# Fused linear attention and feed-forward: PSUM as eight single banks, a filler bank, and a new order table

## The chip, the cores and the metric

The kernel runs on one NeuronCore of a Trainium2 chip. Its engines work side by side, each on its own list of instructions: TensorE (PE in the profile, with its weight loads as PEld), VectorE (DVE), ScalarE (ACT), GpSimd (POOL) and SyncE (SP, which here only starts transfers). TensorE writes its results to PSUM, 16 KB a partition in eight banks of 512 fp32 columns; DVE and ACT read them from there. POOL starts the loads from DRAM that change fp32 to bf16 on the way, SP the transposing transfers and the stores. The metric is the device time of one execution in microseconds.

## The reference

Attention over 8 batches, 8 heads, 576 positions and 64 columns a head, followed by a feed-forward layer over the 4608 rows that come out:

```python
def phi(x):
    proj = np.einsum('bhsd,df->bhsf', x, w_phi)                    # 64 -> 128
    proj = proj - np.max(np.abs(proj), axis=-1, keepdims=True)
    return np.concatenate([np.exp(proj), np.exp(-proj)], axis=-1)
q_p, k_p = phi(q), phi(k)
kv = np.einsum('bhsf,bhsd->bhfd', k_p, v)
z = np.sum(k_p, axis=2)
num = np.einsum('bhsf,bhfd->bhsd', q_p, kv)
den = np.einsum('bhsf,bhf->bhs', q_p, z)[..., None] + 1e-06
x = (num / den) as rows of 512                                     # 8 heads x 64
h = np.maximum(x @ w_in, 0.0)                                      # 512 -> 2048
out = h * h @ w_out                                                # 2048 -> 512
```

## The kernel before

Each batch's K goes through TensorE as 18 blocks of 128 positions in five groups (four of four blocks, one of two, the "rest" of 64 positions a head). The projection `e_kp` (L660) of a group uses half the array's rows for each of two heads. DVE takes the largest absolute value of each row (L595), ACT the two exponentials of either sign (L602) into `kph`. The maximum becomes a factor `em`, by which V is multiplied on DVE (L755, `va`; L738, `var` for the rest). `e_kv` (L776, L781) sums keys times values into `kvs`, eight heads and two signs a batch. Q is projected twice: `e_qm` (L878) for its maximum (DVE, L925) and `e_qp` (L888) for its exponentials (ACT, L915). `e_nd` (L970, and L978 for the rest, which uses half the array's columns) gives numerator and denominator, `e_t` (L1009, L1013 and others on DVE) brings the two signs together in `tmp`, then follow a reciprocal and a multiplication into `xo`.

`xo` is transposed to `xT`: on TensorE (L1083, with a copy out of PSUM) for batches 0 and 1, by a DMA transpose on SP's queue from batch 2 on (L1065, L1068). K and Q themselves go the same way (L630 and L840 on TensorE for batches 0 and 1, L566 and L570 by DMA after that). The feed-forward part runs in chunks of one tile of 128 rows (the first four) or two: `e_hp` (L1133) fills one bank with a group of the first layer, `e_hr` takes the positive part (ACT L1151 or DVE L1153), `e_sq` squares it (ACT L1161 or DVE L1163), `e_op` (L1189) is the second layer, `ot` its copy to SBUF.

PSUM is divided into three tiles `pj` of two banks and two tiles `mo` of one bank. Projections, sums and numerators of whole batches live in `pj`; transposes, the feed-forward and batch 0's sums live in `mo`. A matmul group that writes a tile waits until the last reader of its former content is done.

No planner runs in the kernel. Each piece of work is entered in a list by `add` (or `issue`, two entries for a transfer: start and landing), and `ORDER` gives the sequence in which the entries are emitted; every engine then works through its own part of that sequence. A minus sign takes the second engine that the entry allows. `WARM` gives filler matmuls that stand ahead of an entry (units of 128 columns), written into the tile that the entry is about to use; `e_fill` adds 40 units, and `e_first` 24 at the very start. Without `e_fill`'s own entry, which is not used, `WARM` has 44.

The loads of batch 0 go out on POOL's queue in this order: two pairs of K heads, V whole, the identity matrix (made by POOL itself), K's rest, V's rest, the first half of Q's columns, two parts of w_in, the second half of Q, two parts of w_in, Q's rest; then, once `ones` of batch 0 is done, batch 1's K, the two halves of w_out, and batch 1's Q and V. The other four K heads come in fp32 through SP's queue and are cast. A load waits for a free buffer, and on POOL's queue a transfer also waits for the eighth before it to land.

## Time and profile before

| | us |
|---|---|
| median of 3 runs (lowest, highest) | 360.85 (360.31, 361.56) |
| span of the profiled execution | 358.4 |
| the profiled execution's own time beside its span | not recorded apart from it |
| TensorE busy in the span | 346.4 |
| DVE, ACT, POOL busy in the span | 292.4, 262.9, 58.5 |

The runs time the whole execution; the span goes from the first to the last instruction of one profiled execution, so the median is 2.4 us above it. "Busy" counts the time in which at least one instruction of an engine runs; consecutive instructions overlap a little, so the mean length of one is more than what the next waits for, and the distance from start to start is read from the timeline. The granted clock is TensorE's, as a share of full speed.

### The profile page before, as it was taken

What the parts mean: (1) busy time and instruction counts of PE and PEld (TensorE: products, weight loads), DVE (VectorE), ACT (ScalarE), POOL (GpSimd) and SP (SyncE); (2) the same over time, 40 slices, a digit from 0 to 9 for tenths busy, and PEclk for the clock granted to TensorE, in tenths of its full rate; (3) what the DMA queues carried; (4) which work ended last, traced back from release to release, by engine and by line L of the source; (5) the groups of instructions that cost most, each with busy time, mean ns of one, the idle gap of its engine ahead of it and who ended that gap; (6) DMA issues with size and microseconds to landing.
All of it is one profiled execution on the core that took longest, in us unless ns stands there. A gap on an engine that the chain in (4) does not pass through costs nothing.

```text
span 358.4 us, 9254 instructions
## 1 busy us (share of the span) xinstructions
PE 346.4 (97%) x3860; PEld 239.1 (67%) x3894; DVE 292.4 (82%) x529; ACT 262.9 (73%) x436; POOL 58.5 (16%) x88
## 2 busy tenths in 40 slices
PE   8699999999999999999999999999999999999995
PEld 4378667775776676767576757757685768576754
DVE  5979998889998998788988699979988988591310
ACT  4979997996798774698849883798879867544641
POOL 8643323442160113100220002000000000000000
PEclk9969999999999999999999999999999999999999
DMA  9999999999997499607982194435203001113011
GB/s 161 185 197 207 194 208 141 170 181 187 186 152 138 83 171 150 107 15 145 124 126 53 59 149 96 61 89 82 60 16 88 18 35 48 65 34 88 2 59 59
DMA packets 92281, 39.33 MB, mean 110 GB/s; under 512 B 59728, under 2 KB 87760, under 8 KB 92240
## 3 DMA queue, kind: packets, MB, share of 16 engines
q0 software_dynamic: 42752, 18.09, 42.7%
q1 hardware_dynamic: 49328, 20.59, 28.6%
q8 instruction: 30, 0.49, 0.6%
q10 hardware_dynamic: 160, 0.07, 0.1%
q14 instruction: 11, 0.09, 0.1%
HBM read 36.77 MB, written 9.44 MB: 129 GB/s over the span
## 4 chain that ended last, share of the span: by engine, by line
PE 82%; DVE 8%; ACT 7%; issue 1%; POOL 1%; ACTq 0%; POOLq 0%
PE mo L1133 32%; PE mo L1189 31%; PE pj L781 4%; PE pj L970 4%; ACT kph L602 4%; PE pj L878 3%; PE pj L888 2%; DVE m L595 2%; PE pj L660 2%; DVE tmp L1009 1%; ACT hr L1151 1%; PE pj L776 1%; PE mo L781 1%; DVE va L755 1%; DVE hr L1153 1%
## 5 line engine op out<-in xcount | busy, mean ns | idle before, releaser
L1133 PE MATMUL mo<-xT,win 128*128 128x256 bf16 (+1 forms) x1280 | 139.3, 262 | 0.8 <-ACT hr L1151 0.2
L1189 PE MATMUL mo<-wout,h 128*128 128x512 bf16 (+1 forms) x558 | 131.2, 373 | 1.8 <-issue 0.2
L1133 PEld LDWEIGHTS <-win 128*128 128x128 bf16 x1280 | 111.3, 98 | 19.7 <-issue 4.3
L1189 PEld LDWEIGHTS <-h 128*128 128x128 bf16 x592 | 54.5, 98 | 57.3 <-issue 2.8
L915 ACT ACTIVATE qph<-pj 128x1024 bf16<-128x1024 f32 (+1 forms) x80 | 72.8, 940 | 11.6 <-PE pj L888 11.6
L1151 ACT ACTIVATE hr<-mo 128x512 bf16<-128x512 f32 x99 | 58.7, 598 | 28.2 <-PE mo L1133 27.0
L602 ACT ACTIVATE kph<-pj 128x1024 bf16<-128x1024 f32 (+1 forms) x80 | 71.2, 949 | 6.4 <-PE pj L660 4.9
L1163 DVE TENSOR_TENSOR h<-hr 128x512 bf16<-128x512 bf16 x82 | 33.7, 419 | 22.6 <-ACT hr L1151 22.0
L925 DVE TENSOR_REDUCE mq<-pj 128x8 f32<-128x1024 f32 (+1 forms) x40 | 44.2, 1108 | 4.5 <-PE pj L878 4.4
L595 DVE TENSOR_REDUCE m<-pj 128x8 f32<-128x1024 f32 (+1 forms) x40 | 44.3, 1111 | 3.4 <-ACT kph L602 1.7
L1161 ACT ACTIVATE h<-hr 128x512 bf16<-128x512 bf16 x62 | 38.9, 631 | 8.3 <-DVE hr L1153 7.5
L755 DVE TENSOR_TENSOR va<-vin,em 128x512 bf16<-128x512 bf16 x63 | 40.2, 683 | 0.1
L1153 DVE TENSOR_SCALAR hr<-mo 128x512 bf16<-128x512 f32 x45 | 30.6, 684 | 7.9 <-PE mo L1133 7.4
L417 ACT ACTIVATE ot<-mo 128x512 f32<-128x512 f32 (+1 forms) x24 | 14.0, 585 | 25.1 <-PE mo L1189 25.1
L1009 DVE TENSOR_TENSOR tmp<-pj,e 128x520 f32<-128x520 f32 x31 | 21.1, 692 | 6.1 <-PE pj L970 6.1
L970 PEld LDWEIGHTS <-qph 128*128 128x128 bf16 x512 | 21.9, 98 | 5.4 <-issue 1.5
L1042 DVE TENSOR_TENSOR xo<-tmp,rden 128x512 bf16<-128x512 f32 (+1 forms) x39 | 24.3, 631 | 0.5
L970 PE MATMUL pj<-kvs,qph 128*128 128x65 bf16 x512 | 24.4, 194 | 0.2
L781 PEld LDWEIGHTS <-kph 128*128 128x128 bf16 x512 | 21.5, 101 | 0.3
L1013 DVE TENSOR_TENSOR tmp<-pj,tmp 128x520 f32<-128x520 f32 x31 | 21.2, 692 | 0.5 <-PE pj L970 0.4
L781 PE MATMUL pj<-va,kph 128*128 128x65 bf16 x448 | 18.4, 194 | 0.0
L467 POOL DMA_DIRECT2D vin<-in_v_dram x8 | 7.2, 895 | 68.5 <-DVE va L755 63.1
(75 smaller groups left out, 268.5 us busy)
## 6 DMA issues: line engine op xcount, KB each, us to landing
out_dram<-ot SPq DMA_DIRECT2D x31, 256.0 KB, 2.4
vin<-in_v_dram POOLq DMA_DIRECT2D x8, 512.0 KB, 9.0
kin<-in_k_dram POOLq DMA_DIRECT2D x7, 512.0 KB, 11.9
qin<-in_q_dram POOLq DMA_DIRECT2D x7, 512.0 KB, 10.3
win<-in_moe_w_in_dram POOLq DMA_DIRECT2D x4, 512.0 KB, 10.1
...
xT<-xo SPq DMA_TRANSPOSE x36, 2.6
```

The source lines that it names most:

```text
L595: nc.vector.tensor_reduce(out=st["m"].rearrange("p (n c) -> p c n", c=2)[:, :, n0 : n0 + n], in_=st["pj", g][:, :, :n], axis=AX.X, op=ALU. ...
L602: nc.scalar.activation(out=st["kph"][:, s, n0 : n0 + n].rearrange("p n c f -> p c n f"), in_=st["pj", g][:, :, :n], func=ACT.Exp, scale=1. ...
L755: nc.vector.tensor_tensor(out=st["va"][:, s, gs, 0:D], in0=tiles["v", b].rearrange("p h i d -> p (h i) d")[:, gs, :], in1=st["em"][:, s, g ...
L781: nc.tensor.matmul(out=kv[:, sum_of(h) - 2 * prs[0], :], lhsT=st["kph"][:, s, 2 * h + i // 2, i % 2, :], rhs=st["va"][:, s, h * NI + i, :] ...
L915: nc.scalar.activation(out=st["qph", pt][:, s, half, n0 : n0 + n], in_=in_, func=ACT.Exp, scale=1.0 - 2.0 * s)
L925: nc.vector.tensor_reduce(out=st["mq", pt][:, half, n0 : n0 + n], in_=in_, axis=AX.X, op=ALU.max, apply_absolute_value=True)
L970: nc.tensor.matmul(out=nps[:, n + 4 * (ab or 0), :], lhsT=qph[:, s, half, sl, :], rhs=kvs[:, s, sum_of(sl), :], start=True, stop=True)
L1133: nc.tensor.matmul(out=hp[:, mi, :], lhsT=win[:, kc, mc * P : (mc + 1) * P], rhs=st_x[c][:, kc, 0:nt, :], start=kc == kcs[0] and (ab is No ...
L1151: nc.scalar.activation(out=out_, in_=in_, func=ACT.Relu)
L1153: nc.vector.tensor_scalar(out=out_, in0=in_, scalar1=0.0, scalar2=None, op0=ALU.max)
L1161: nc.scalar.activation(out=out_, in_=hr, func=ACT.Square)
L1189: nc.tensor.matmul(out=st["op"], lhsT=hst["h2"][:, mc, tt * P : (tt + 1) * P], rhs=wout[:, mc, cols], start=(mc == 0), stop=(mc == KC2 - 1))
```

## The change

- **PSUM.** `r_pj` and `r_mo` become one ring `r_ps` of eight single banks. All that took a two-bank tile takes two banks: K's and Q's projections, with one reduction and one exponential a sign for each bank; the sums in two halves of four heads; the numerators in groups of four heads. `e_qm` and `e_qp` are entries of their own in all batches, so that the table may place them apart.
- **Fillers.** `e_first` takes one bank, `spare`, which goes back to the ring with the first group of the first layer. All fillers are matmuls into that bank. `e_fill` goes; `WARM` has 187 units, all ahead of the first layer.
- **w_phi** comes in one transfer that doubles it over the partitions; `w2` has one plane, one cast, and no clearing.
- **Batch 0's loads.** POOL's queue: identity, K heads, V in two halves of four heads, V's rest, first half of Q, two parts of w_in, second half of Q, two parts of w_in, Q's rest, batch 1's K. Then come the seven multiplications that POOL now does in batch 0 (in the table's order: `va` negative sign groups 2, positive 2, one half of `var`, `va` positive 3, negative 0, 1 and 3), then K's rest of batch 1, w_out, batch 1's Q and V. K's rest of batch 0 comes in fp32 on SP's queue and is cast. The second set of loads no longer waits for `ones`. The first sum of batch 0 needs the first three of the seven, the last sum all seven.
- **Batch 1's `xo`** goes by DMA transpose like the later ones (`PE_X` names batch 0 alone).
- **Squares** are taken of two groups at once (1024 columns), except in the last chunk; `r_hr` has three double buffers.
- **`load_gate`**: from batch 3 on, the loads of a batch wait for the first `xo` of two batches before, by a small copy on POOL into `mark`.
- **`e_one`** may run on ACT instead of DVE.
- **`ORDER`** has 2084 entries instead of 1718. Of its relus ACT has 107 (99 before) and DVE 37 (45); of its squares ACT has 43 (62) and DVE 33 (82).

The diff, cut:

```diff
-WARM = {44: 7, 54: 10, 58: 6, 62: 2, 74: 13, 93: 4, 117: 5, 139: 2, 149: 8}
+WARM = {47: 3, 57: 6, 49: 1, 64: 9, 51: 1, 71: 22, 85: 30, 134: 21, 139: 13, 138: 12, 148: 14, 147: 8, 110: 1, 112: 3, 189:
+    4, 197: 13, 158: 1, 217: 3, 166: 2, 176: 3, 170: 11, 172: 6}
...
-    XB_IN, XB_X = 2, 2
+    XB_IN, PE_X = 2, [(0, pt, half) for pt in range(3) for half in range(2)]
...
-    r_pj = Ring("pj", 3, [P, 2, 4, P], F32, pool=ps)
-    r_mo = Ring("mo", 2, [P, 4, P], F32, pool=ps)
+    r_ps = Ring("ps", 8, [P, 4, P], F32, pool=ps)
...
-    r_hr = Ring("hr", 4, [P, 512], BF16)
+    r_hr = Ring("hr", 3, [P, 2, 512], BF16)
...
-        for half in range(2):
-            nc.scalar.dma_start(out=wst[half * Dh : (half + 1) * Dh], in_=w_phi)
+        nc.scalar.dma_start(out=wst, in_=w_phi.unsqueeze(0).to_broadcast([2, Dh, Fd]))
...
     def e_first(op):
-        warm(r_pj.tile(op)[:, 0], WARM_UP, zero)
...
+        spare["t"] = r_ps.tile(op)
+        fill(WARM_UP, zero)
+
+    def fill(n, with_):
+        for m in [4] * (n // 4) + ([n % 4] if n % 4 else []):
+            nc.tensor.matmul(out=spare["t"][:, :m], lhsT=with_, rhs=with_.unsqueeze(1).to_broadcast([P, m, P]),
                              start=True, stop=True)
...
+                o, d = plan.issue("sw", 1, key, {"pool": (0.92, 0.95)}, emit_v, "half", (), [] if o_v else [r_in["v"].slots],
+                                  after=[o])
...
+            for par in range(2):
+                lock = Lock()
+
+                def e_red(op, g=g, n0=n0, n=n, par=par):
+                    nc.vector.tensor_reduce(
+                        out=st["m"].rearrange("p (n c) -> p c n", c=2)[:, par, n0 : n0 + n], in_=st["pj", g, par][:, :n],
+                        axis=AX.X, op=ALU.max, apply_absolute_value=True)
...
+                for s in range(2):
+                    def e_exp(op, g=g, n0=n0, n=n, par=par, s=s):
+                        nc.scalar.activation(out=st["kph"][:, s, n0 : n0 + n, par, :], in_=st["pj", g, par][:, :n],
+                                             func=ACT.Exp, scale=1.0 - 2.0 * s)
...
-            va_on = {"dve": (0.6, 0.69)}
+            va_on = {"dve": (0.6, 0.69)} if b else {"dve": (0.6, 0.69), "pool": (1.04, 1.05)}
...
-                        nc.vector.tensor_tensor(
+                        eng = nc.gpsimd if op.engine == "pool" else nc.vector
+                        eng.tensor_tensor(
                             out=st["va"][:, s, gs, 0:D],
                             in0=tiles["v", b].rearrange("p h i d -> p (h i) d")[:, gs, :],
                             in1=st["em"][:, s, gs].unsqueeze(2).to_broadcast([P, 8, D]), op=ALU.mult)
...
-            parts = [range(0, 2), range(2, 4)] if b == 0 else [range(4)]
+            parts = [range(0, 2), range(2, 4)]
...
-                    o_qm = o_qp = add(key, {"pe": (tm[0] + tq[0], tm[0] + tq[1])}, e_qmp, need + [o_w2],
-                                      [hm, hq] + first, give=qT_give + qT_give, after=[o_mq], mode="row")
...
+                o_qm = add(key, {"pe": mm(P, w * (1 + split))}, e_qm, need + [o_w2], hm + first[:1], give=qT_give,
+                           after=[o_mq], mode="row")
+                o_qp = add(key + (0.1 if b else 2), {"pe": mm(128 * w, 1 + split)}, e_qp, need + [o_w2], hq + first[1:],
+                           give=qT_give, after=[o_q0], mode="row")
...
+                        for hg in (0, 1) if ab is None and pt < 2 else (0,):
+                            heads = (2 * ab, 2 * ab + 1, 2 * ab + 4, 2 * ab + 5) if first_tile else range(4 * hg, 4 * hg + 4)
+                            holds = [Hold(r_ps.slots) for _ in range(1 if pt < 2 else 2)]
...
+            pair = c < len(CHUNKS) - 1
+            at, upto = (g % 2, g % 2) if pair else (0, 1)
...
+    def load_gate(b, key):
+        o_xo, owner, st, name = firsts[b - 2]
+
+        def emit(_):
+            nc.gpsimd.tensor_copy(out=mark[:, b : b + 1], in_=st[name][:, 0, 0:1])
...
+            o_before = o_second if b == 2 else load_gate(b, first_key(b) - 46.0)
...
-            o_second = first_loads(SECOND, kv_ops["ones"], 16)
+            o_second = first_loads(SECOND, o_first_loads, 16)
...
     for o in plan.order():
+        if o.warm:
+            fill(o.warm, ident)
```

468 lines of the change are left out of this document (212 added, 256 removed), and 193 rows, old and new, of tables (ORDER, WIRE).

## The prediction

> **What bounds the kernel now.** I read the page first, then stretches, then TensorE's order in time.
>
> ```profile
> span 358.4 us, 9254 instructions
> PE 346.4 (97%) x3860; PEld 239.1 (67%) x3894; DVE 292.4 (82%) x529; ACT 262.9 (73%) x436; POOL 58.5 (16%) x88
> ```
> ```profile
> 0.00:28.40 28.40, 23.21 (x250) 14.72 (x250) 22.40 (x45) 20.27 (x44) 18.25 (x32) 0.88 1.29 182
> 28.40:320.00 291.60, 288.60 (x3377) 201.14 (x3406) 261.23 (x466) 227.39 (x367) 40.25 (x57) 1.00 0.73 110
> 320.00:358.40 38.40, 34.60 (x237) 23.28 (x238) 8.81 (x20) 15.22 (x27) 0.00 (x0) 1.00 0.20 55
> 60.00:80.00 20.00, 19.42 (x261) 14.29 (x261) 15.77 (x28) 17.96 (x28) 7.18 (x10) 1.00 1.55 164
> 10.00:20.00 10.00, 6.73 (x66) 4.15 (x65) 9.72 (x19) 10.00 (x27) 6.18 (x11) 0.84 1.37 193
> 20.00:30.00 10.00, 9.82 (x154) 8.07 (x154) 8.21 (x18) 7.01 (x12) 5.66 (x8) 0.82 1.39 199
> ```
>
> Each row is a stretch, its length, then busy time of PE, PE weight loads, DVE, ACT and POOL, granted clock, DMA share, GB/s. Between 28.4 and 320 us TensorE is idle for 3.0 of 291.6 us. So from the first matmul of the first layer (at 28.41, below) the kernel is TensorE's instruction stream, and only three things can move the end: when that stream begins, what is in it, and new holes in it. DVE is busy for 90% of that stretch and ACT for 78%. Ahead of it, 10 to 20 us, ACT and DVE are full, TensorE is not, and its clock drops.
>
> ```profile
> 7.11 1.23 DVE L595 TENSOR_REDUCE m<-pj 128x8 f32<-128x1024 f32 x1 [0.75 <-PE pj L660]
> 8.36 2.85 ACT L602 ACTIVATE kph<-pj 128x1024 bf16<-128x1024 f32 x3 [0.34 <-DVE m L595]
> 10.33 1.23 DVE L595 TENSOR_REDUCE m<-pj 128x8 f32<-128x1024 f32 x1 [0.21 <-ACT kph L602]
> 10.98 0.89 POOL L470 DMA_DIRECT2D qin<-in_q_dram  x1 [1.85 <-DMA vin<-in_v_dram]
> 14.08 0.61 PE L840 MATMUL mo<-ident,qin 128*128 128x128 bf16 x8
> 16.66 0.93 PE L878 MATMUL pj<-w,qT 64*128 64x128 bf16 x8 [1.97 <-DVE m L595]
> 22.67 0.65 PE L781 MATMUL mo<-va,kph 128*128 128x65 bf16 x8
> 24.28 0.41 PE L781 MATMUL mo<-va,kph 128*128 128x65 bf16 x8
> 28.41 1.96 PE L1133 MATMUL mo<-xT,win 128*128 128x128 bf16 x32
> ```
>
> These are rows of the timeline (start, length, engine, line; in brackets the idle time before and what ended it). The two-bank tile `pj` is passed whole between DVE and ACT: each waits for the other's read of it, which single banks relax. At 22.67 eight matmuls take 0.65 us, at 24.28 the same eight take 0.41: the clock. From the start of the last sum of batch 0 (24.28) to the first layer (28.41) it is 4.1 us of latency.
>
> **The change, part by part.**
>
> *Start of the stream.* The new POOL order is identity, K heads, two V halves, V rest, then the loads of Q, w_in and batch 1's K, and then seven multiplies of batch 0 (six `va`, one `var`), the last of them needed by the last sum. The row at 10.98 shows an issue waiting for a transfer eight issues older. Batch 1's K is eight issues behind the first Q half, which has landed by 14.08; so POOL reaches the multiplies at 14.1 + 0.9 (one issue, the same row) = 15.0 us. No trace row shows such a multiply on POOL.
>
> ```profile
> L755 DVE TENSOR_TENSOR va<-vin,em 128x512 bf16<-128x512 bf16 x63 | 40.2, 683 | 0.1
> masks.py:199 POOL TENSOR_SCALAR_AFFINE_SELECT ident<-ident 128x128 bf16<-128x128 bf16 x1 | 0.3, 287 | 0.1
> L750 ACT ACTIVATE va<-vin,em 128x64 bf16<-128x64 bf16 x8 | 2.1, 417 | 0.0
> L1083 PE MATMUL mo<-ident,xo 128*128 128x128 bf16 x36 | 3.9, 220 | 0.1
> h<-in_k_dram SPq DMA_DIRECT2D x2, 256.0 KB, 3.0
> ```
> ```profile
> 67.86 0.58 ACT L417 ACTIVATE qT<-mo 128x512 bf16<-128x512 bf16 x1
> 68.34 4.67 ACT L602 ACTIVATE kph<-pj 128x1024 bf16<-128x1024 f32 x5
> 93.05 1.22 DVE L925 TENSOR_REDUCE mq<-pj 128x8 f32<-128x1024 f32 x1
> 94.18 0.69 DVE L1013 TENSOR_TENSOR tmp<-pj,tmp 128x520 f32<-128x520 f32 x1
> 94.79 0.68 DVE L1153 TENSOR_SCALAR hr<-mo 128x512 bf16<-128x512 f32 x1
> 95.39 1.89 DVE L755 TENSOR_TENSOR va<-vin,em 128x512 bf16<-128x512 bf16 x3
> 24.91 0.76 DVE L1001 TENSOR_TENSOR tmp<-pj,e 128x260 f32<-128x260 f32 x2 [0.58 <-PE pj L970]
> ```
>
> From start to start, ACT takes 0.48 us for 512 columns (67.86 to 68.34) and 0.91 for 1024 (five in 4.67, of which the last runs out over about 1.0); DVE takes 1.13 for a reduction of 1024 (93.05 to 94.18), 0.61 for 520 columns, 0.60 for 512 (94.79 to 95.39), and for 260 about 0.35 (two in 0.76, the last running out over 0.42).
> The same multiply takes 0.68 us on DVE, one end; a one-input pass of POOL over 128 columns takes 0.29 us, so four times that, 1.15, is the other, and as a fixed part is counted four times it may hold for two inputs too; the diff's own planner figure is 1.04. I take 1.1, nearest the POOL row: 15.0 + 7 x 1.1 = 22.7 us for the last sum instead of 24.28, and with the 4.1 us behind it the first layer starts at 26.8 instead of 28.4: **-1.6**. It can't come much sooner than 25: ACT's 20.3 us of work ahead of that point lose 2.1 (L750) and gain the eight exponentials of 0.48 that the new table puts ahead of it, 22.0 in all, and the first keys take 3.0 us to land. DVE has 22.4 us there, loses six multiplies of 0.68 and gains four reductions of 0.6. So the ends are -3.4 (start at 25) and, with dear multiplies, a loss (first rival).
> The Trainium skill, "GPSIMD Engine Reference", section 3.1, counts about 2.6 cycles an element for a two-input operation; at its 1.2 GHz that is 1.11 us for 512, an estimate, and the sum would stay. No run here shows it.
>
> *The rest of the start* is hidden by that chain. The single w_phi load, one cast instead of two and one clearing less save ACT's and DVE's tenths where neither is waited for last; the identity comes earlier; the V half adds one issue of 0.9 us on POOL, and K's rest leaves POOL with two of 0.64 (SP issues it, 1.0 us, with nothing else to do, and a cast of some 0.35 goes to DVE). Fillers grow from 84 to 187 units; they fill waits, and at half clock they would cost (second rival).
>
> *What is in the stream.*
>
> ```profile
> 205.13 0.41 PE L970 MATMUL pj<-kvs,qph 128*128 128x65 bf16 x8
> 205.37 1.04 PE L1133 MATMUL mo<-xT,win 128*128 128x256 bf16 x8
> 206.34 0.40 PE L660 MATMUL pj<-w,kT 64*128 64x128 bf16 x8
> 206.67 1.92 PE L1133 MATMUL mo<-xT,win 128*128 128x256 bf16 x16
> 208.85 1.05 PE L1133 MATMUL mo<-xT,win 128*128 128x256 bf16 x8
> 209.74 1.89 PE L1189 MATMUL mo<-wout,h 128*128 128x512 bf16 x7
> 211.79 0.38 PE L888 MATMUL pj<-qT,w 64*128 64x512 bf16 x2
> 212.10 0.44 PE L978 MATMUL pj<-kvs,qph 128*64 128x65 bf16 x16
> ```
>
> Eight L1133 matmuls take 0.97 us until an L660 starts (205.37 to 206.34), but 0.89 until an L1189 (208.85 to 209.74). L660, L878 and L888 use half the array's rows, L978 half its columns; a change of shape costs about 0.09, and coming back the same (L660's eight are four concurrent pairs, 4 x 0.056 = 0.22, and take 0.33 until the next L1133). Call it 0.097. Walking both tables from the first L1133 and counting neighbours of different shape on TensorE gives 112 changes before and 82 after, because K and Q projections now stand together more often: 30 x 0.097 = **-2.9**. Ends: 30 x 0.08 = 2.4 and 30 x 0.11 = 3.3.
> Batch 1's attention output goes through DMA transposes instead of TensorE: 18 of the 36 L1083 matmuls go. By 3.9/36 it is 0.108 each with the drain, by L1133's pace (0.109 for 256 columns) 0.055; in a full stream the pace counts: **-1.0** (end -1.9). It adds six DMA transposes on SP, where batch 2 and later have theirs. Batch 2's way is hidden today behind the groups in front; without that cover one late tile would cost the landing of 2.6 us (first row below).
> The split of the sums, the numerators and the score banks adds no matmul: they stay 8 per group or become 2 x 4 in the same shape, cost nothing of TensorE's. Ahead of the first layer the new table puts one L888 pair (211.79 to 212.10, less the change: 0.21), two transposes (0.11) and twelve L970 matmuls (eight take 0.24 from 205.13: 12 x 0.03) more than the old: 0.7 less behind it, **-0.7**.
>
> *New holes.*
>
> ```profile
> xT<-xo SPq DMA_TRANSPOSE x36, 2.6
> kin<-in_k_dram POOLq DMA_DIRECT2D x7, 512.0 KB, 11.9
> kT<-kin SPq DMA_TRANSPOSE x6, 7.7
> ```
>
> Two halves of 512 columns cost ACT 2 x 0.48 - 0.91 = 0.05 more than one of 1024, and DVE's reduction 2 x 0.60 - 1.13 = 0.07; two of 260 cost DVE 2 x 0.35 - 0.61 = 0.09 more than one of 520. Split are 160 exponentials (+8 us of ACT), 80 reductions and 62 numerator steps (+11 of DVE). Squares in pairs spare some 0.07 each, 68 times (an estimate from the same fixed part, -5), batch 1's copies go, and the table moves squares from DVE (82 to 33, most of them double) to ACT, and relus too (99 to 107). DVE then falls to about 86% in the stretch and ACT rises to about 85%, still under DVE's 90% of today, which leaves TensorE 99% busy. Only at 60 to 80 us, where today DVE 15.8 and ACT 18.0 of 20 go with 0.58 us of TensorE idle, does the new table ask for about as much as both can give. I put **+1.5** for holes there; ends 0 and +7.
> The new GpSimd mark makes the loads of batch 3 and later wait for the first output of two batches before. What is queued behind it is loads alone. By the two tables' TensorE work, the tightest gate stands 24 us ahead of its batch's first projection; load and transpose need 11.9 + 7.7 = 19.6, so nothing, and if late the shortfall.
>
> *Sum.* -1.6 - 0.7 - 2.9 - 1.0 + 1.5 = -4.7: a span of 353.7. The profiled execution's own time isn't given apart from its span of 358.4; the median of the runs, 360.85, lies 2.4 above the span, which I take as what lies around it: **356.1 us**.
>
> **The rivals.**
> 1. *Slower: POOL's multiplies are dear.* The place is the seven-long chain ahead of the last sum of batch 0. The price is 7 us for each us per multiply above 1.1. All else gives -3.1, so it decides from 1.1 + 4.7/7 = 1.8 us. At 2.3 the time is 356.1 + 8.4 = 364.5. For it: no row of POOL has two inputs, and DVE is busy for 9.7 of the 10 us beside it. Against: the POOL row.
> The Trainium skill's "GPSIMD Engine Reference", section 1, says that GpSimd shares its SBUF interface with VectorE, with contention from DVE instructions of two SBUF inputs; that speaks against this change, and no run here shows both at once.
> 2. *The clock drops again at the start.* Today it does (0.84, 0.82) after a thin stretch. Half clock over some 7 us, as the slow L781 rows show, takes 3.4 us of work: 359.5. For it: the start still waits for ACT. Against: twice the fillers, in the waits.
> The Trainium skill, "TensorE: Matmul & The Clock Gate", Part 1, puts the clock down after an idle window of about 3.4 us; by it 1.97 us of idle would not be enough alone, and the trace's drop came after several such waits.
> 3. *ACT and DVE become the bound.* If each 20 us stage from 40 to 320 loses 0.6 us more, 14 x 0.6 = 8.4 replaces the 1.5: 363.0; break-even with before is at 0.44. For it: both engines at 85%. Against: DVE's 90% today.
> 4. *The start does not move:* the second Q half or ACT ends last anyway; without the 1.6, 357.7.
>
> **How the numbers follow.** Forecast 0.50 (own range 352.5 to 358.5), rival 1 0.13, 2 0.11, 3 0.14, 4 0.12. About 0.3% (1.1 us) is what a measurement can tell from no change. Faster: forecast, rival 4 and half of 2, with a little of 3: 0.69. Same: 0.08, from 2 and 3. Slower: 0.23, from 1, 3 and a bad 2. The range goes down to 351.5 (start at 25, no holes) and up to 364, past rival 3; about 0.06 and 0.11 lie outside.
>
> **What would show it.** The first L1133 near 26.8; the seventh POOL multiply ending near 22.7, each at 1.1; granted clock 1.00 from 10 to 30; the 18 L1083 of batch 1 gone; TensorE idle from the first layer to 320 no more than 4.5 us; DVE under 88% there. Wrong would make it: multiplies at 1.8 or more, a first layer after 30, or TensorE waiting on ACT in every stage.

## The result and the profile after

The changed kernel takes 398.36 us (median; 394.53 to 401.12) against 360.58 for the kernel before in the same comparison. The ratio is 1.101 [1.0945, 1.1074]: it is 10% slower, where 1.3% faster was forecast. The profiled execution took 397.9 us, 1.8 above its span (2.4 was assumed). The slowest of its four executions, 401.12, counts as a slow one and is left out of the ratio; without it the median is 397.9, so differences taken from 398.36 below may be half a microsecond too large.

The page of the changed kernel: span, engines, the costliest group, and the issues of the transposes of `xo`.

```profile
span 396.1 us, 9565 instructions
PE 361.6 (91%) x3897; PEld 246.3 (62%) x3897; DVE 290.7 (73%) x592; ACT 280.8 (71%) x603; POOL 66.9 (17%) x97
L1115 PE MATMUL ps<-xT,win 128*128 128x256 bf16 (+1 forms) x1280 | 145.2, 269 | 19.7 <-DMA xT<-xo 16.0
xT<-xo SPq DMA_TRANSPOSE x42, 2.5
```

TensorE is busy 91% instead of 97%, and no other engine has taken its place: DVE is at 73%, ACT at 71%. The first layer (L1133 before, L1115 now) names what TensorE waits for: 16.0 us on DMA transposes of the attention output. The median landing of these is 2.5 us, about as before (2.6). That median hides what happened.

Stretches of the changed kernel (start and end, length, then PE, PE loads, DVE, ACT, POOL busy, granted clock, DMA share, GB/s); the first two are split at the first matmul of the first layer. The DMA share adds up all packets under way, so it can pass 1.

```profile
0.00:36.52 36.52, 30.24 (x287) 17.05 (x288) 27.03 (x50) 22.80 (x57) 27.28 (x38) 0.86 1.19 171
36.52:396.10 359.58, 331.35 (x3616) 229.30 (x3612) 263.66 (x542) 258.01 (x546) 39.58 (x59) 0.97 0.60 94
10.00:20.00 10.00, 10.00 (x81) 5.28 (x78) 8.46 (x15) 8.36 (x25) 6.29 (x9) 0.87 1.42 200
20.00:30.00 10.00, 8.02 (x81) 5.33 (x80) 8.63 (x14) 5.26 (x14) 9.88 (x11) 0.66 1.18 149
60.00:80.00 20.00, 19.24 (x308) 13.51 (x306) 18.40 (x41) 16.63 (x40) 6.03 (x10) 1.00 0.43 70
80.00:100.00 20.00, 14.40 (x126) 10.47 (x126) 11.43 (x23) 10.63 (x24) 0.54 (x1) 0.83 1.13 127
120.00:140.00 20.00, 17.57 (x161) 11.89 (x160) 15.80 (x33) 17.17 (x38) 4.61 (x7) 1.00 1.31 172
160.00:180.00 20.00, 15.89 (x133) 11.12 (x132) 10.21 (x21) 7.20 (x15) 1.02 (x2) 0.91 1.01 143
220.00:240.00 20.00, 16.77 (x157) 11.44 (x156) 13.95 (x31) 15.24 (x37) 3.02 (x5) 0.91 1.08 161
260.00:280.00 20.00, 13.18 (x115) 7.45 (x114) 11.37 (x25) 12.02 (x29) 2.87 (x5) 0.83 1.21 172
```

The spans differ by 396.1 - 358.4 = 37.7 us, and the rows split them:

- *Start:* the first layer begins at 36.52 instead of 28.41, **+8.1**.
- *Idle time behind it:* 359.58 - 331.35 = 28.2 us, where the two rows of before gave (291.60 - 288.60) + (38.40 - 34.60) = 6.8: **+21.4**. Most of it lies in five stages: the rows at 80, 120, 160, 220 and 260 have 100 - 77.81 = 22.2 of the 28.2. Transposes of `xo` are 16.0 of it; the two largest waits beside them are 3.2 us for ACT's `kph` (at 224.55) and 2.4 us for the transpose of K's rest (at 132.76).
- *Half clock behind it:* four of these rows have a clock below 1.00, 20 x (0.17 + 0.09 + 0.09 + 0.17) = **10.4** us of work lost (an estimate, since the clock counts while TensorE waits, too).
- *What is left:* 37.7 - 8.1 - 21.4 - 10.4 = **-2.2**: TensorE's own work did get cheaper. As a remainder it carries the error of the 10.4.

Compare the DMA share at 60 to 80 us: 1.55 before, 0.43 now, and 1.13 behind it, at 80 to 100. The loads of batch 3 have moved later, all together. One hole shows what they meet. From the timelines of the changed kernel, GpSimd's queue first, then SyncE's, then TensorE's:

```profile
72.79 0.19 POOL L1219 COPY mark<-xo 128x1 bf16<-128x1 bf16 x1 [21.38 <-DVE xo L1031]
73.28 0.90 POOL L487 DMA_DIRECT2D qin<-in_q_dram  x1 [0.30 <-issue]
74.17 0.89 POOL L487 DMA_DIRECT2D kin<-in_k_dram  x1
...
77.46 0.96 POOL L487 DMA_DIRECT2D vin<-in_v_dram  x1
```
```profile
76.53 1.36 SPq L1057 DMA_TRANSPOSE xT<-xo  x1
```
```profile
85.25 3.57 PE L1115 MATMUL ps<-xT,win 128*128 128x256 bf16 x16 [5.13 <-DMA xT<-xo]
```

The gate's copy of `mark` opens at 72.79 and three loads of 512 KB leave within five microseconds. A transpose of `xo` leaves at 76.53, into the middle of them. The first layer of that tile stands still until 85.25, and its sixteen matmuls then take 3.57 us where they took 1.92 in the kernel before (206.67): half clock. The waits of TensorE and the last line of the view of the tile `xT` give the size:

```profile
PE ps L1115 <- DMA xT<-xo: 16.0, 4, 6.8
```
```profile
DMA to landing us min/median/max: 2.3/2.5/8.6
```

Four waits, 16.0 us, the longest 6.8; a landing of up to 8.6 where the median is 2.5.

### The profile page after: what moved, and what is told of

Read it like the earlier page. It is cut to its first block, busy times and chain, and to the rows that moved or that the text cites. A ratio compares the mean times of both kernels' runs of the same rounds, so it can differ in the third digit from the quotient of the medians.

```text
span 396.1 us, 9565 instructions
## 1 busy us (share of the span) xinstructions
PE 361.6 (91%) x3897; PEld 246.3 (62%) x3897; DVE 290.7 (73%) x592; ACT 280.8 (71%) x603; POOL 66.9 (17%) x97
## 5 line engine op out<-in xcount | busy, mean ns | idle before, releaser
L1115 PE MATMUL ps<-xT,win 128*128 128x256 bf16 (+1 forms) x1280 | 145.2, 269 | 19.7 <-DMA xT<-xo 16.0
L1115 PEld LDWEIGHTS <-win 128*128 128x128 bf16 x1280 | 114.7, 100 | 40.4 <-DMA xT<-xo 11.6
L1183 PE MATMUL ps<-wout,h 128*128 128x512 bf16 (+1 forms) x592 | 134.5, 374 | 0.8 <-ACT h L1154 0.2
L1138 ACT ACTIVATE hr<-ps 128x512 bf16<-128x512 f32 x107 | 62.9, 612 | 54.5 <-PE ps L1115 53.0
L906 ACT ACTIVATE qph<-ps 128x512 bf16<-128x512 f32 (+1 forms) x160 | 79.1, 575 | 9.3 <-PE ps L892 9.2
L632 ACT ACTIVATE kph<-ps 128x512 bf16<-128x512 f32 (+1 forms) x160 | 78.5, 582 | 8.4 <-PE ps L687 7.8
L624 DVE TENSOR_REDUCE m<-ps 128x4 f32<-128x512 f32 (+1 forms) x80 | 47.4, 629 | 7.2 <-ACT kph L632 3.8
L913 DVE TENSOR_REDUCE mq<-ps 128x4 f32<-128x512 f32 (+1 forms) x80 | 47.8, 629 | 3.7 <-PE ps L883 3.2
L1154 ACT ACTIVATE h<-hr 128x1024 bf16<-128x1024 bf16 (+1 forms) x43 | 42.8, 1004 | 3.5 <-DVE hr L1140 2.9
L996 DVE TENSOR_TENSOR tmp<-ps,tmp 128x260 f32<-128x260 f32 x64 | 26.1, 423 | 10.5 <-PE ps L961 8.5
L961 PE MATMUL ps<-kvs,qph 128*128 128x65 bf16 x512 | 28.9, 196 | 0.5 <-DVE mq L913 0.4
```

Source lines behind the costliest of these rows:

```text
L624: nc.vector.tensor_reduce(out=st["m"].rearrange("p (n c) -> p c n", c=2)[:, par, n0 : n0 + n], in_=st["pj", g, par][:, :n], axis=AX.X, op= ...
L632: nc.scalar.activation(out=st["kph"][:, s, n0 : n0 + n, par, :], in_=st["pj", g, par][:, :n], func=ACT.Exp, scale=1.0 - 2.0 * s)
L906: nc.scalar.activation(out=st["qph", pt][:, s, half_, h0 : h0 + nh_], in_=st["pq", pt, pi][bank][:, :w], func=ACT.Exp, scale=1.0 - 2.0 * s)
L913: nc.vector.tensor_reduce(out=st["mq", pt][:, half_, h0 : h0 + nh_], in_=st["pm", pt, pi][bank][:, :w], axis=AX.X, op=ALU.max, apply_absol ...
L961: nc.tensor.matmul(out=nps[0][:, n, :], lhsT=qph[:, s, half, sl, :], rhs=kvs[:, s, sum_of(sl), :], start=True, stop=True)
L1115: nc.tensor.matmul(out=hp[:, mi, :], lhsT=win[:, kc, mc * P : (mc + 1) * P], rhs=st_x[c][:, kc, 0:nt, :], start=kc == 0, stop=kc == KC1 - 1)
```

## The experiments

The theory I formed from this: transposes of `xo` by DMA are late when they fly beside the loads, and the change brings the two together in three ways (batch 1's output by DMA, the gate, the new table's later loads). Its rivals: GpSimd's multiplies and the clock at the start; the transposes' place in SyncE's queue, whatever the loads carry.

### Is it the gate, and is it the multiplies?

**e1.** The gate's copy reads a constant instead of the attention output, so it opens at once:

```diff
-            nc.gpsimd.tensor_copy(out=mark[:, b : b + 1], in_=st[name][:, 0, 0:1])
+            nc.gpsimd.tensor_copy(out=mark[:, b : b + 1], in_=ident[:, 0:1])
```

> The changed kernel with one word altered: the small GpSimd copy ahead of the loads of batch 3 and later reads a constant instead of the attention output, so those loads wait for a free buffer alone. Order table and queues are the changed kernel's. Theory A (the gate lets the loads of a batch go all at once and late, and their bytes hold up the DMA transposes of xo): TensorE's idle time between the first layer and 380 us falls from about 24 us to under 6, the clock stays at 1.00 there, the wait of L1115 for xT (16.0 us) falls under 4, and the time is about 366 us (397.9 less 22 of idle less 10 of half clock). The first layer stays at 36.5. Rival B (SP's queue order in the new table, long transposes of Q and K ahead of those of xo, makes the holes): the holes stay and the time is above 388 us.

Measured: 385.65 us (385.06 to 386.74), 1.0712 [1.0662, 1.0763]. The open gate is worth 398.36 - 385.65 = 12.7 us, a third of the loss, and neither theory's number. The timeline of GpSimd in this run shows why it is no more:

```profile
72.73 0.89 POOL L487 DMA_DIRECT2D qin<-in_q_dram  x1 [21.79 <-PE ps L848]
```

The loads of batch 3 leave at the same time as in the changed kernel. Now it is Q's load that stands at the head of the queue and waits 21.79 us for its buffer, which the transposes on TensorE (L848) have to leave; K (73.62) and V stand behind it. V's main load leaves at 76.91, where it left at 77.46. The later batches gained (TensorE at 260 to 280: 19.49 of 20, against 13.18).

**e2.** The same, with the seven multiplies of batch 0 back on DVE (a minus in the table stands for the second engine):

```diff
-    72, -95, 28, 98, -100, 106, -108, 34, 134, 135, 38, 87, 136, 137, 139, 141, 140, -96, 3, 91, 99, 94, 79, 102,
+    72, 95, 28, 98, 100, 106, 108, 34, 134, 135, 38, 87, 136, 137, 139, 141, 140, 96, 3, 91, 99, 94, 79, 102,
...
```

> As the run with the open gate, and batch 0's seven multiplications go back from GpSimd to VectorE at the same places of the order table. Theory A (the start was lost because GpSimd's multiplications and VectorE's work slow each other, so that VectorE falls behind between 18 and 26 us): the seven take 0.68 us each on VectorE, its casts of em go back from about 1.0 to 0.2 us, the first L1115 comes at about 33 us instead of 36.5, and the time is about 3 us under that of the open gate alone. Rival B (the start was lost elsewhere: w_phi's cast at 6.2 us, K's rest, two drops of the clock): the first L1115 stays within 1 us of 36.5 or comes later, since VectorE has 4.8 us more to do ahead of it.

Measured: 385.25 us (383.06 to 387.35), 1.071 [1.063, 1.079]; first layer at 35.5, against 36.2 in e1. The multiplies on GpSimd neither win nor lose anything that can be measured. Why they win nothing is in DVE's timeline. First the changed kernel, with GpSimd's multiplies beside it, then e2 without them:

```profile
18.93 1.03 POOL L751 TENSOR_TENSOR var<-vrest,em 64x512 bf16<-64x512 bf16 x1
19.93 5.22 POOL L769 TENSOR_TENSOR va<-vin,em 128x512 bf16<-128x512 bf16 x4
...
17.99 2.07 DVE L425 CAST var<-em 64x8 bf16<-64x8 f32 x2
20.07 1.49 DVE L769 TENSOR_TENSOR va<-vin,em 128x512 bf16<-128x512 bf16 x1
21.48 0.68 DVE L624 TENSOR_REDUCE m<-ps 128x4 f32<-128x512 f32 x1
...
22.68 1.00 DVE L425 CAST va<-em 128x16 bf16<-128x16 f32 x1
...
24.28 1.42 DVE L751 TENSOR_TENSOR var<-vrest,em 64x512 bf16<-64x512 bf16 x1
```
```profile
19.59 0.36 DVE L425 CAST var<-em 64x8 bf16<-64x8 f32 x2
19.97 0.69 DVE L769 TENSOR_TENSOR va<-vin,em 128x512 bf16<-128x512 bf16 x1
...
23.44 0.20 DVE L425 CAST va<-em 128x16 bf16<-128x16 f32 x1
...
24.24 0.69 DVE L751 TENSOR_TENSOR var<-vrest,em 64x512 bf16<-64x512 bf16 x1
```

The two small casts, the multiply, the third cast and the last multiply take 2.07 + 1.49 + 1.00 + 1.42 = 5.98 us beside GpSimd's multiplies and 0.36 + 0.69 + 0.20 + 0.69 = 1.94 without: 4.0 us more, while DVE is spared seven multiplies of 0.60 (the pace of the prediction's rows), 4.2. A reduction that reads PSUM (L624) takes 0.68 in both. The Trainium skill, "SBUF — State Buffer", section "SBUF: two separate sides", says that DVE and GpSimd take turns at one pair of ports, for the whole of an instruction, and that only DVE instructions with two SBUF inputs or in a two-port mode are held up; the trace agrees, down to the cast of 64x8 that lasts as long as one GpSimd multiply (2.07 for two, 1.03 for the row at 18.93), if the casts run in such a mode, which no trace here shows.

### Is it the bytes?

**e3.** The changed kernel, gate and table kept, but the main loads of batches 3 to 7 fetch a fourth of their bytes; GpSimd sets the rest of the tile to one. What is left out is three quarters of the inputs of these batches: the result isn't the reference's.

```diff
+            if b >= 3:
+                cols = slice(0, 1)
+                nc.gpsimd.memset(tiles[name, b][:, :, 1:NI], 1.0)
```

> The changed kernel, gate kept, but the main loads of batches 3 to 7 bring a fourth of their bytes (GpSimd sets the other three fourths to one), so the result of those batches is not the reference's. Theory A (the bytes of the bunched loads hold up the transposes of xo): the wait of L1115 for xT falls from 16.0 us to under 4, transposes of xo land in about 2.5 us also right behind the loads, and the time is 365 to 375 us. Rival B (the waiting comes from the transposes of Q and K in SP's queue, or from loads that are released too late): the holes stay and the time is above 385 us.

Measured: 375.59 us (one run), 22.8 below the changed kernel and just above theory A's range (its wait under 4 us is missed, too: 5.5). From the waits of TensorE, the view of `xT`, and the timeline of this run:

```profile
PE ps L1118 <- DMA xT<-xo: 5.5, 4, 2.0
```
```profile
DMA to landing us min/median/max: 2.3/2.5/5.3
```
```profile
81.21 1.91 PE L1118 MATMUL ps<-xT,win 128*128 128x256 bf16 x16 [0.89 <-DMA xT<-xo]
```

The same transposes at the same places of the same queues: their longest landing falls from 8.6 to 5.3, the wait from 16.0 to 5.5, and the hole at 80 is 0.89 us instead of 5.13, with the sixteen matmuls at full pace. So it is the loads that make the transposes late, not the order of SyncE's queue alone. Two things about the loads differ here, though: each memset takes some 1.4 us ahead of its load, so those of batch 3 also leave later, Q's at 74.42, K's at 76.62 and V's at 81.24, which is 1.1, 2.4 and 3.8 us. Fewer bytes and later departures are not parted by this run.

**e4.** The kernel before with a gate put into it: behind the first attention output of batches 1 to 4, GpSimd copies a column of it, and the loads of three batches later (the edit to the table) stand behind that copy.

```diff
+                        if 1 <= b <= 4 and b not in gated:
+                            gated.add(b)
+                            nc.gpsimd.tensor_copy(out=mark[:, b : b + 1], in_=xo[:, 0, 0:1])
```

> The kernel before, with a gate put into it: a small GpSimd copy of the first xo of batches 1 to 4 stands right behind that xo in the order, and the loads of batches 4 to 7 stand behind the copy of three batches before (the old table needs them too early for a distance of two). Nothing else is changed. Theory A (a gate that bunches the loads costs TensorE time whatever the table): TensorE idles for xT or kT at some of the four places, and the time is 364 to 380 us. Rival B (three batches of distance leave the loads room, and a gate alone costs nothing): 360 to 362 us. Either way the page shows whether loads released together slow a transpose of xo beyond 4 us.

Measured: 362.8 us (361.57 to 363.98), 1.0062 [1.0033, 1.0091]. TensorE waits 2.3 us for `xT` in two places: 1.4 us in the stage 140 to 160 (busy 18.43 of 20) and 0.8 at 200.86. A gate in the old table costs little, between what the two theories expected. It is looser than the change's (three batches instead of two), and there is more slack behind it: read from the traces, from the last transpose of a chunk to its first layer it is 4.9 to 9.8 us in the kernel before (mostly 6.5), and in the new table, where no wait stretches it, 3.0 to 5.9 (mostly 4). With 6.5 in hand a landing of 6.9, the worst of this run (the transpose that leaves at 193.85), costs the 0.8 us; with 4 it would be a hole. That the slack is the reason is argued, not shown: the run doesn't part it from the gate's distance.

### Batch 1's output by DMA

**e10.** The kernel before, one number changed: batch 1's attention output goes through the DMA transposes, like batch 2's. (Two minus signs of the table, at 316 and 324, are dropped with it.)

```diff
-    XB_IN, XB_X = 2, 2
+    XB_IN, XB_X = 2, 1
```

> The kernel before, with one number changed: batch 1's xo goes to xT by DMA transpose instead of TensorE and a copy (18 matmuls less). The old order table places the first layer for a short wait. Theory A (the transposes of batch 1 stand in the time of the loads and land late, 5 us or more instead of 2.5): TensorE idles for xT at several tiles between 50 and 110 us, 8 us or more in all, the clock drops there, and the time is 368 us or more. Rival B (the prediction's step: 1.0 us saved, one late tile at most for 2.6): 358 to 362 us.

Measured: 378.02 us (376.12 to 378.58), 1.0479 [1.0437, 1.0521]: **+17.8 us** from the step that the prediction had at -1.0. TensorE's timeline, its waits, and the view of `xT`:

```profile
86.34 6.21 PE L1133 MATMUL mo<-xT,win 128*128 128x256 bf16 x32 [13.47 <-DMA xT<-xo]
```
```profile
PE mo L1133 <- DMA xT<-xo: 15.5, 3, 13.5
```
```profile
DMA to landing us min/median/max: 2.3/2.9/10.7
```

13.47 us of standing still, and 32 matmuls in 6.21 us instead of 3.8 (2 x 1.92 by the row of before). In the kernel before this stage had a DMA share of 1.55 and cost nothing (TensorE idle for 0.58 of 20 us): TensorE waited for none of its transfers. Not all of the 13.47 us is flight, as the next run shows.

**e14.** e10 with the loads of batches 2 to 7 cut to a fourth as in e3 (again three quarters of these inputs are left out).

```diff
+            if b >= 2:
+                cols = slice(0, 1)
+                nc.gpsimd.memset(tiles[name, b][:, :, 1:NI], 1.0)
```

> The kernel before with batch 1's xo by DMA transpose, and the main loads of batches 2 to 7 bring a fourth of their bytes (GpSimd sets the other three fourths to one), so the result of those batches is not the reference's. Theory A (the bytes of the loads are what makes the transposes of batch 1's xo land late): the wait of 13.5 us at 73 to 86 us shrinks to under 4, and the time is 358 to 365 us instead of 378. Rival B (a transpose by DMA is late there for another reason, SP's queue or the transposes of K and Q): the wait stays above 8 us and the time above 370.

Measured: 365.43 us (one run), just above theory A's range: 12.6 of the 17.8 are gone. TensorE's waits:

```profile
PE mo L1136 <- DMA xT<-xo: 4.2, 3, 1.9
```

Three waits again, 4.2 instead of 15.5, the first of them 1.8 us where it was 13.47; the longest landing is 5.3, as in e3. With e3 this is shown twice, in two kernels: the traffic of the loads makes the transposes late. As in e3 the memsets also let the loads leave 1 to 4 us later (the three from 68.08 on at 69.31, 72.73 and 76.15), so the bytes are the likely part of it, not the only one that was changed.

The lateness has two parts. In e10 the first transpose of `xo` stands in SyncE's queue behind a transpose of K, which is slow itself. SyncE's queue in e10, then in e14:

```profile
68.61 5.76 SPq L566 DMA_TRANSPOSE kT<-kin  x1
74.46 2.99 SPq L1065 DMA_TRANSPOSE xT<-xo  x1
```
```profile
64.86 1.97 SPq L569 DMA_TRANSPOSE kT<-kin  x1
68.97 1.20 SPq L1068 DMA_TRANSPOSE xT<-xo  x1
```

The next transpose of `xo`, the one that the first layer waits for here, leaves at 78.87 and lands after 7.4 us in e10; in e14 it leaves at 72.31 and lands after 2.4. So 6.6 us of the hole came from the wait in the queue and 5.0 from the flight, and both go with the small loads.

**e12.** The other way round: the changed kernel with only batch 1's output back on TensorE (seven entries of the table move with it, by up to 44 places).

```diff
-    XB_IN, PE_X = 2, [(0, pt, half) for pt in range(3) for half in range(2)]
+    XB_IN, PE_X = 2, [(b, pt, half) for b in range(2) for pt in range(3) for half in range(2)]
```

> The changed kernel, gate and loads as they are, with batch 1's xo through TensorE and a copy again: one part undone. Theory A (batch 1's xo by DMA, among the loads of batch 3, makes the hole of 5.1 us at 80 to 85 us and the half clock behind it, and the other holes are the other gates'): that hole goes, the others stay, and the time is 5 to 9 us below 398. Rival B (the gate's loads then meet the next transposes, of Q and K, and the hole only moves): less than 3 us.

Measured: 395.31 us (392.32 to 398.12), 1.0944 [1.0843, 1.1045], 3 below the changed kernel, and the two intervals overlap. One stretch of it:

```profile
80.00:100.00 20.00, 18.40 (x189) 14.25 (x190) 17.82 (x36) 17.12 (x39) 0.31 (x1) 1.00 0.65 91
```

The hole at 80 is closed (18.40 at full clock, 14.40 at 0.83 before the edit), and the later ones remain or grow (TensorE is busy 17.0 us of 20 at 120 to 140, and 17.2 at 140 to 160, where it was 19.95). The gate, which still releases each batch's loads in one bunch, is the likely reason. So 17.8 in the old table is not 17.8 in the new one: the prices of these steps don't add.

### The loads' place in the table

**e5.** The gate open as in e1, and thirty entries of the table, the loads of batches 3 to 7, moved up to where their buffers come free, so that Q's load no longer holds the others back.

```diff
-    -183, 252, 256, 263, 269, 259, 264, 131, 253, 205, 1466, 267, 221, 1467, 206, 257,
+    -183, 252, 597, 256, 263, 269, 259, 264, 131, 253, 205, 1466, 267, 221, 1467, 206, 257,
...
             o_before = o_second if b == 2 else load_gate(b, first_key(b) - 46.0)
+            o_before = o_second
```

> The changed kernel without the gate's dependence, and in the order table alone the load entries of batches 3 to 7 moved up to where a buffer is free (30 entries; no other entry moves). With the gate open the first loads of batch 3 still left POOL at 72.7 us, behind Q's load at the head of the queue. Theory A (loads come late and together, behind the gate and behind each other in POOL's queue, and meet the transposes of xo): TensorE's wait for xT falls from 12.0 us to under 5, the clock stays at 1.00 from 40 us on, and the time is 368 to 376 us instead of 385.65. Rival B (the bytes meet the transposes of xo whenever they come, since batch 1's xo now takes the DMA way in the time when the loads run): the holes move, and the time stays above 381.

Measured: 379.18 us (378.1 to 380.35), 1.0528 [1.046, 1.0596], 6.5 below e1 and between the two theories' ranges. TensorE's wait for `xT` is 6.5 us in two waits (12.0 in e1), and the stage at 80 to 100 goes from 14.31 us busy at clock 0.83 to 17.43 at 1.00. From GpSimd's timeline of this run, two of the same three loads:

```profile
65.41 0.90 POOL L485 DMA_DIRECT2D kin<-in_k_dram  x1 [11.05 <-DMA kT<-krest]
...
67.51 0.92 POOL L485 DMA_DIRECT2D vin<-in_v_dram  x1
```

K and V leave eight to nine microseconds earlier than in e1, so less of them is still under way when `xo` is transposed; Q's load has its old time (73.16). A hole of 2.1 us is left at 82 and one of 4.4 us at 157.

**e6.** e5 with batch 1's output on TensorE (again with seven more entries of the table moved):

```diff
-    XB_IN, PE_X = 2, [(0, pt, half) for pt in range(3) for half in range(2)]
+    XB_IN, PE_X = 2, [(b, pt, half) for b in range(2) for pt in range(3) for half in range(2)]
```

> As the run with early loads, and batch 1's xo goes through TensorE and a copy again (18 matmuls of L1074 more, five DMA transposes and the rest tile's two less). Theory A (one of the dear holes is batch 1's xo, which is transposed by DMA while loads of batches 3 and 4 run): the wait of TensorE for xT at 80 to 100 us goes, the clock there is 1.00, and the time falls by 3 us or more below that of early loads alone. Rival B (early loads already spare that transpose): no gain, and about 1 us more for the 18 matmuls.

Measured: 376.58 us (374.4 to 379.06), 1.0451 [1.0379, 1.0522]; wait for `xT` 3.9 us, first layer at 34.6. In order, then: gate 12.7, place of the loads 6.5, batch 1's output 2.6, together 21.8 of the 37.8 us that the medians differ. What stays above the kernel before is 376.58 - 359.99 = 16.6; 6.2 of it is the start (34.6 instead of 28.41), 3.9 the wait for `xT`, and the rest is in smaller waits and in the clock, which no run here takes apart. A caution for all that follows: e1, e5 and e6 have the same instructions in the same order up to the first layer, and it begins at 36.2, 36.6 and 34.6. A first layer read from one trace is good to about 2 us, and the last 2.6 may be partly that.

### The start

**e7.** e2 without the 187 filler units.

```diff
-WARM = {47: 3, 57: 6, 49: 1, 64: 9, 51: 1, 71: 22, 85: 30, 134: 21, 139: 13, 138: 12, 148: 14, 147: 8, 110: 1, 112: 3, 189:
-    4, 197: 13, 158: 1, 217: 3, 166: 2, 176: 3, 170: 11, 172: 6}
+WARM = {}
```

> The run with the open gate and the multiplications on VectorE, and without the 187 units of fillers ahead of the first layer (the 24 at the very start stay). Theory A (the fillers stand in TensorE's line and at half clock hold up the work behind them, 3.4 us between 19.4 and 25.5): the first L1115 comes at about 32.5 us instead of 35.5. Rival B (the fillers keep the clock up, or fill waits for VectorE and ScalarE only): the first L1115 stays at 35.5 or comes later, and the half clock lasts longer than the 3 us and 6 us it has with them.

Measured: 385.5 us (one run) against 385.25; first layer at 35.8 against 35.5. Without the fillers nothing changes that these runs could tell.

**e8.** e6 with the multiplies on DVE, no fillers, and some fifty entries of batch 0 put in another order in the table: V's multiplies and the sums ahead of Q's projections and exponentials, as the kernel before has them. The first of the entries that moved:

```diff
-    -22, 25, -26, 63, 60, 49, 50, 64, 68, 51, -52, 70, 69, 66, 61, 55, 53, 71, 77, 54, 73, 56, 78, 74, 76, 58, 59,
-    82, 65, 84, 80, 83, 32, 92, -93, 75, 85, 89, 86, 88, -97, 72, -95, 28, 98, -100, 106, -108, 34, 134, 135, 38,
+    -22, 25, 63, 60, 49, 50, -26, 64, 68, 51, -52, 70, 69, 66, 61, 55, 53, 71, 77, 54, 73, 56, 78, 74, 76, 58, 59,
+    82, 65, 84, 80, 83, 32, 28, 34, 92, -93, 75, 72, 98, 85, 89, 86, 95, 94, 106, 100, 99, 101, 134, 135, 136, 137,
...
```

> The run with early loads and batch 1's xo on TensorE, without fillers, and some 50 entries of the order table of batch 0 put in another sequence (no entry added or removed): K's rest is cast behind the copy of kT; the seven multiplications are on VectorE; the maxima of K, the factors and both halves of var come ahead of Q's maxima, and the four sums come ahead of Q's second pair of projections. Theory A (the start was lost in the order on VectorE and TensorE: the first sum waits for var's second half at 25.3 us, behind a maximum of Q and other sums' factors, and Q's second projections stand ahead of the sums): the first sum comes at about 21 us instead of 25.4, and the first L1115 at 31 to 33 us instead of 35.5; the time falls 2 to 4 us below 376.58. Rival B (VectorE's and ScalarE's work ahead of the first layer is the bound in any order, or the half clock): the first L1115 stays at 34.5 or later.

Measured: 378.22 us (376.79 to 379.62), 1.0495 [1.0458, 1.0531]. The sums run from 18.9 to 24.4, as early as in the kernel before, and the first layer still begins only at 34.1.

**e9.** e8 with the multiplies on GpSimd:

```diff
-    95, 94, 106, 100, 99, 101, 134, 135, 136, 137, 139, 88, 87, 110, 79, 102, 103, 107, 104, 108, 67, 138, 91, 90,
-    112, 81, 97, 96, 114, 105, 109, 141, 111, 116, -113, -115, 117, 145, 142, 140, 146, 143, 144, 148, 147, 38, 3,
+    -95, 94, 106, -100, 99, 101, 134, 135, 136, 137, 139, 88, 87, 110, 79, 102, 103, 107, 104, -108, 67, 138, 91, 90,
+    112, 81, -97, -96, 114, -105, -109, 141, 111, 116, -113, -115, 117, 145, 142, 140, 146, 143, 144, 148, 147, 38, 3,
```

> The same, with the seven multiplications on GpSimd as in the changed kernel. Theory A (GpSimd's multiplications and VectorE slow each other, so that they spare VectorE nothing): each takes 1.0 to 1.3 us, VectorE's small casts beside them take several times their 0.2 us, and the first layer comes no earlier than in the run on VectorE. Rival B (they spare VectorE 4 us): the first layer comes 2 us or more earlier than there.

Measured: 379.02 us (one run); first layer at 36.9, against 34.1 with DVE. The 2.8 us are a little over what one trace can tell, and 0.8 of it shows in the time. The lengths are the ones known from above: GpSimd's multiplies take 1.04 for the first and 5.56 for five, and DVE's pair of small casts 2.02 instead of 0.36.

**e11.** e8 with the fillers of the changed kernel:

```diff
-WARM = {}
+WARM = {47: 3, 57: 6, 49: 1, 64: 9, 51: 1, 71: 22, 85: 30, 134: 21, 139: 13, 138: 12, 148: 14, 147: 8, 110: 1, 112: 3, 189:
+    4, 197: 13, 158: 1, 217: 3, 166: 2, 176: 3, 170: 11, 172: 6}
```

> The run with the start's order changed, and with the 187 units of fillers in front of the same entries as in the changed kernel. In that run the sums ended at 24.4 us, as in the kernel before (24.7), but the first layer came 9.7 us later, not 4.1, and TensorE ran at half clock from 7 to 25 us and again from 32 us. Theory A (half clock takes the rest): the clock is 1.00 over most of 10 to 24 us, and the first layer comes at 31 us or earlier instead of 34.1. Rival B (behind the sums ScalarE's exponentials of Q, 14 in a row from 25.4 to 32.3, end last, whatever the clock; fillers stand in TensorE's line): the first layer stays at 33.5 or later.

Measured: 374.01 us (one run), the best of the changed kernel's variants, 14 above the kernel before. The granted clock is 1.00 from 10 to 40 us. TensorE's timeline, then ACT's:

```profile
23.78 0.41 PE L789 MATMUL ps<-va,kph 128*128 128x65 bf16 x8
...
34.72 1.95 PE L1113 MATMUL ps<-xT,win 128*128 128x128 bf16 x32
```
```profile
25.47 3.02 ACT L904 ACTIVATE qph<-ps 128x512 bf16<-128x512 f32 x6
29.05 4.03 ACT L904 ACTIVATE qph<-ps 128x512 bf16<-128x512 f32 x8 [0.56 <-PE ps L890]
```

The last sum starts at 23.78 at full clock (0.41, not 0.65), and the first layer 10.9 us later. In the kernel before it was 4.1. So half clock isn't what makes the start late. It isn't free behind the start: e11 differs from e8 by the fillers alone, and with a first layer that is no earlier it is 4.2 us faster, since e8's clock is 0.66 at 30 to 40 us and 0.86 at 140 to 160 where e11's is 1.00. (One run of e11; the waits of the two traces differ, too.) Between the two stand ACT's exponentials of Q. Here is what the kernel before had of them ahead of its first layer, from ACT's timeline:

```profile
19.52 2.00 ACT L915 ACTIVATE qph<-pj 128x1024 bf16<-128x1024 f32 x2
...
25.38 1.02 ACT L915 ACTIVATE qph<-pj 128x1024 bf16<-128x1024 f32 x1 [0.17 <-PE pj L888]
...
26.77 1.03 ACT L915 ACTIVATE qph<-pj 128x1024 bf16<-128x1024 f32 x1
```

Four of 1024 columns, which is eight of 512 (a fifth starts at 28.29, beside the first layer). In e11 sixteen of 512 stand there (two before the rows above, then six and eight), and in the changed kernel sixteen as well. Fourteen of them form one stretch, from 25.5 to 33.1, behind the last sum. The stream behind the first layer has no less to do for it: in e11 it takes 372.0 - 34.72 = 337.3 us where it took 330.0, with 14.3 us of TensorE idle instead of 6.8 (TensorE busy 323.0, as before). The largest of its waits behind the first layer is again for `xT` (3.3 us, of which 2.95 at 154.49); the others are for `xo` on DVE (1.5) and below 1 us.

**e13.** e11 with the numerators of the first tile and its first layer ahead of the next tile's Q work (entries 156 to 171), and 158 filler units.

```diff
-    148, 147, 38, 3, 120, 122, 124, 126, 121, 153, 154, 152, 150, 151, 186, 187, 184, 128, 130, 132, 149, 185, 156,
-    125, 157, 189, 194, 193, 188, 196, 195, 42, 133, 424, 426, 197, 200, 158, 203, 159, 160, 161, 425, 436, 46,
+    148, 147, 156, 157, 158, 159, 160, 161, 162, -163, 164, 165, 166, 167, 168, 169, 170, 171, 1461, 38, 1463, 3,
+    120, 122, 124, 126, 121, 153, 154, 152, 150, 151, 186, 187, 184, 128, 130, 132, 149, 185, 125, 189, 194, 193,
...
```

> The run with the start's order changed and with fillers, and one thing more in the order table: the numerators of batch 0's first tile, what follows them (division, transposes) and the first groups of the first layer come ahead of Q's projections, maxima and exponentials for the second half of that tile and for the next tile (fillers that would stand behind the first layer are dropped: 158 units instead of 187). In that run the sums ended at 24.2 us at full clock and the first layer still came at 34.7. Theory A (ScalarE's and VectorE's work for the next half tile and tile, put ahead by the new table, is the rest of the start's loss): the first layer comes at 29 to 31 us. Rival B (the chain from the last sum to the first layer is longer in single banks and quarter steps, in any order): 33 us or later. The time follows only in part, since work put off comes back in the stream.

Measured: 384.14 us (381.45 to 386.35), 1.0699 [1.0648, 1.0751]: ten slower than e11, although the first layer begins at 31.1. The stretch behind it:

```profile
30.00:40.00 10.00, 6.42 (x81) 5.40 (x81) 5.52 (x12) 5.09 (x11) 2.21 (x4) 0.83 1.32 203
```

The next tile's Q work was indeed what held the first layer: with it behind, the layer begins 3.6 us earlier. But TensorE is busy for 6.42 of these 10 us and falls to half clock for a part of them, since what it does next needs just that Q work (its waits in this run: `qT` 2.8 us, `qph` 1.3, `mq` 1.0). The time of the first layer is the wrong thing to judge a start by, unless the same work stands ahead of it. Why the kernel before goes on without such a gap with half as many of Q's exponentials in front is not separated by these runs: the table's order and the passing of single banks are both candidates, and that stays open.

## Why the prediction was wrong

- **"Batch 2's way is hidden today behind the groups in front; without that cover one late tile would cost the landing of 2.6 us": failed, and the dearest step when taken alone.** The eighteen matmuls went, as counted (L1074 x18 in the groups of the changed kernel, L1083 x36 before). But I priced the late tile by the median landing. The trace of before had the other end too, in the view of `xT`:

```profile
DMA to landing us min/median/max: 2.3/2.6/7.6
```

  And the stage of batch 1's output had a DMA share of 1.55, in a row that I had quoted for its DVE and ACT columns. In isolation (e10) the step costs 17.8 us, with a wait of 13.47: 6.6 us of late departure behind a transpose of K, for which the sum had no term at all, and a landing of 7.4. The cover was there for batch 2; for batch 1 I named none, and still took the best case. In the changed kernel undoing this step alone gains only 3 us, with intervals that overlap (e12), so there the next step is the larger one.

- **"What is queued behind it is loads alone ... so nothing": failed, and the largest step in the changed kernel itself.** The loads are indeed all that is queued, and their own batch hardly waits for them (2.4 us once, for K's rest). I asked only whether they come in time, not what they meet. Released together, they meet the transposes of `xo` of the batch that is running (12.7 us by e1, 6.5 more by the place in the queue, e5), and e3 shows that it is these loads: with a fourth of their bytes, leaving a little later, the wait falls from 16.0 to 5.5.

- **The start, "-1.6": failed, +8.1.** The price of a multiply on GpSimd was right (1.1 against 7.1 / 6 = 1.2 in the row below). GpSimd reached them at 16.92 and not at 15.0: it waited for ACT's `em`, not for a transfer. They end at 25.1 and not at 22.7. That is at most 2.4 of the 9.7 us by which the first layer missed 26.8.

```profile
L769 POOL TENSOR_TENSOR va<-vin,em 128x512 bf16<-128x512 bf16 x6 | 7.1, 1209 | 3.2 <-ACT em L718 3.1
```

  The failing part is "with the 4.1 us behind it the first layer starts at 26.8". From the timeline of TensorE in the changed kernel, the last sum and the first layer:

```profile
32.86 0.41 PE L791 MATMUL ps<-va,kph 128*128 128x65 bf16 x8
...
36.52 0.67 PE L1115 MATMUL ps<-xT,win 128*128 128x128 bf16 x9
```

  The last sum stands at 32.86, nearly eight microseconds after the last multiply, with Q's projections and exponentials among the sums. The 3.7 us behind it look like the 4.1 of before, but by chance: in e11 the last sum is at 23.78 and the gap 10.9. I had counted the eight further exponentials, as a total: 22.0 us of ACT's work ahead of 25 us. The total was right (22.80 in the row 0:36.52). Their place was not: most of them come behind the sums, in a row, and the latency behind the last sum, taken over from the old table, had no room for them.

- **TensorE's work, "-0.7 - 2.9 - 1.0": about half.** -4.6 was forecast, -2.2 measured. The shape changes are as I had them: by the records, neighbours of different shape from the first layer on fall from 112 to 82, and a first-layer matmul takes 0.205 us from start to start where half rows follow, 0.109 where its own kind does; 30 x 0.096 = 2.9. What took some of it back shows in e11, whose clock is 1.00 throughout: the 256 matmuls of Q's projection for its maximum (`w,qT`) fill 10.0 us from start to start, 7.6 in the kernel before. Why they do is not shown.

- **Rival 1, dear multiplies: its mechanism, not its price.** At 1.2 us each they are below the 1.8 from which it was to decide. The contention that it named is real and took from DVE what the move spared it, but the start is late with the multiplies on either engine (e1 36.2, e2 35.5, where 28.41 was the mark).

- **Rival 2, the clock at the start: it dropped further** (0.87 and 0.66 at 10 to 30, where 1.00 was to show a right forecast), but e11 at 1.00 is no earlier. For the start it is a symptom; behind it, it is part of the 4.2 us between e8 and e11.

- **Rival 3, ACT and DVE as the bound: no.** ACT's work came out near the forecast, 280.8 us busy instead of 262.9 (+18, where 85% for 78% of 291.6 us meant +20), DVE's did not, 290.7 instead of 292.4 (-2, where 86% for 90% meant -12), but neither is what TensorE mostly waits for. At 60 to 80 us, the stage for which I had put +1.5 in, TensorE is idle 0.76 us instead of 0.58.

- **The range** has a slip of its own: its low end of 351.5 is put down to "start at 25, no holes", which alone gives 352.8; the other 1.3 are the ends of the shape changes and of the transposes.

- **What no rival covered** is that a transfer of which only the bytes or the time move can make another late. None of the four priced a transfer that comes late beside other transfers; the DMA columns of the rows were left unread.
